# Retention attention and a routed expert layer in one kernel: order of loads, list reads and weight splits around the passage between them

## The chip, the cores and the metric

One core of a Trainium2 chip runs the whole program. The metric is the time of one execution in microseconds (us) of device time, lower is better. TensorE (PE in the profile) multiplies, PEld is its weight load, VectorE is DVE, ScalarE is ACT, GpSimd is POOL, SyncE is SP and issues most of the DMAs.

## What is computed

A decayed linear attention over 4 batches, 8 heads, 768 positions and 64 features; then each of the 3072 tokens goes to one of 16 experts, a two-layer network of width 1024, chosen by a group and then within the group:

```python
state = gamma * state + einsum('bhd,bhe->bhde', k[:, :, t], v[:, :, t])
y[:, :, t] = scale * einsum('bhd,bhde->bhe', q[:, :, t], state)
x = y.transpose(0, 2, 1, 3).reshape(B * S, H * D)
g = argmax(x @ w_group)
e = argmax(x @ w_expert[g])
out = softmax_weight(g) * softmax_weight(e) * (relu(x @ w1[g, e]) @ w2[g, e])
```

## The kernel before

**Attention** is twelve steps (`NS2`), the loop of `attention` (L901). A step i takes 128 positions of two batches and handles its operands as chunks. It has these TensorE groups: the scores of step i+1 (`score_mm`, L227, tile `sh`), the part of the outputs from the running state (`state_out`, L278, tile `op`), the part from the values (`value_out`, L291), the state update (`state_mm`, L253, tile `stp`, from the scaled values `vs` and the transposed keys `kk`), the router's logits of step i-1 (`logits_mm`, L310) and the transposes of that step's x (`trans_mm`, L322), which ScalarE copies to `xr` (L329) and SP writes to `xd` in HBM (L332). VectorE masks the scores (L239) and scales the outputs with the decays `gx` to `xt` (`out_x`, L303). The decays of the first position block come by DMA (`decay_load`, L190), those of later ones are made by GpSimd from the ones before (L195). GpSimd also scales the values (`vprep`, L187).

In steps 9 and 10 the transposed keys of the next step aren't made by TensorE but loaded (`KEYED`, L204), into a tile with one buffer, so the load waits until the state update of the step itself is done. All loads, the writes of x and the reads of lists are issued in the order of the program on SP's one queue, and each may wait there.

**Routing** (`route`, L335) runs for batches of four chunks, cut in pieces by `yield` which `route_steps` places between the attention's groups: argmaxes and one-hot rows `oh` on VectorE (L358 to L374, with one exponential on ScalarE, L362), the ranks by TensorE (L399, L401), slots from the ranks (L407 to L419), and the tokens' weights (`weights`, L382 to L394, into `src`). `enlist` (L440) then has GpSimd write each chunk's tokens to the lists `meta` in HBM by an indirect DMA. The lists of experts 0 and 1 are cut in two: an early part, complete after twelve chunks, and the rest.

**Experts** come in "units". The four static ones are `ua` and `va` (early lists of experts 0 and 1) and `ub`, `vb` (their later tokens, same weights); 14 units for the experts in order of their list's length follow. For each, `listed` reads the list (L630, SP, tile `mt`), `gather` gets the tokens (L640, GpSimd, tile `xg`), `xtrans` transposes them (L658, tile `tpx`) and splits them into an fp16 part on ScalarE (L660) and a bf16 rest on VectorE (L661); `layers` multiplies with three products for each pair of parts (L681, tile `hps`; L713 and others, tile `yps`) and `scatter` writes the rows out (L814). Weights are loaded as f32 (`wload`, or in quarter tiles `wload_part`, L604, tile `wf`) and split by `wsplit`: high part `wh` on ScalarE (L616), rest `wl` on VectorE or, for `ua`, on GpSimd (L618).

**What sets the order.** The schedule is manual: every engine runs its instructions in the order in which the Python code emits them. `attention` calls `beside(i, place)` at five places of a step, place -1 at its head, 0 after the decays, 2 ahead of the values' outputs, 1 after the outputs are scaled, 3 after the transposes of x; and `extra(i)` at its end. `beside` holds what is done for the experts during the attention: loads of `ua`'s and `va`'s parts, the early lists' reads (step 9), their gathers (step 10), the transposes of `ua` (step 11) and some splits. `NEXT` says which quarter tiles of `va` are loaded in which step. After the loop `run` (L1056 to L1094) emits the passage: last logits, three low splits, `first(2)` (the first pieces of `ua`'s layers, which `self.first` holds), the last x, the last batch's routing, ranks between further pieces of `ua`, the remaining list entries, the transposes of `va`, the reads of the later lists, the ordering of the experts (`order`, L451) and then `va`, `ub`, `vb`, during which the transposes of `ub` wait for its gather.

PSUM has banks by tag: `big` (three), `tra`, `mid` (two), `sta`, `log`. The four attention banks `sh` are the three `big` and the `tra` one; `sta` holds the running state until step 10, and serves unit transposes later.

## Time and profile before

| | us |
|---|---|
| median of 3 runs | 429.47 |
| lowest, highest | 427.44, 431.81 |
| profiled execution | 429.22 |
| its span, first to last instruction | 427.5 |
| TensorE busy in the span | 407.7 |
| VectorE, ScalarE, GpSimd busy | 289.3, 223.5, 176.4 |

The profile is of one execution. The span is what the trace covers; the execution's own time is 1.7 us longer. A busy TensorE is not TensorE at its peak, since the ends of matmuls are modelled. Idle time of an engine that nothing waits for costs nothing. [...]

### The profile page before, as it was taken

Reading aid. Unit: us, or ns where it says so; the run is one execution under the profiler, and the core shown is the slowest. Engines: PE = TensorE matmul, PEld = TensorE weight load, DVE = VectorE, ACT = ScalarE, POOL = GpSimd, SP = SyncE. Lnnn points to the kernel's source line nnn. Section 1 sums busy time; section 2 is a strip of 40 time slices with the busy share of each in tenths; the row PEclk is TensorE's granted clock in tenths of the full one; section 3 lists DMA queues with packets and bytes.
Section 4 is the critical chain, followed back from the end, with each engine's and each line's share of the span. In section 5 each row is a group of like instructions: output and inputs, shape, how many; then the busy total and the mean of one; then the engine's idle time right before and its main releaser. Section 6 shows DMA issues by size and latency. Waiting matters only on the chain.

```text
span 427.5 us, 13524 instructions
## 1 busy us (share of the span) xinstructions
PE 407.7 (95%) x5721; PEld 335.3 (78%) x5721; DVE 289.3 (68%) x473; ACT 223.5 (52%) x342; POOL 176.4 (41%) x153
## 2 busy tenths in 40 slices
PE   8899999899898999999999999999999999999991
PEld 4798989787765778585979788897978879878791
DVE  4455675578683557676898786867768778687620
ACT  2134435445523556555556566666766657667520
POOL 4445679648877021440508052442513415222001
PEclk9999999999999999999999999999999999999997
DMA  8999999998445967776776876879778797786000
GB/s 277 366 306 314 379 310 322 350 251 265 164 102 191 340 250 229 247 260 233 254 245 219 281 269 244 291 256 282 267 288 286 272 299 280 278 321 241 26 9 34
DMA packets 36913, 107.94 MB, mean 253 GB/s; under 512 B 13784, under 2 KB 13784, under 8 KB 29684
## 3 DMA queue, kind: packets, MB, share of 16 engines
q1 hardware_dynamic: 25908, 89.76, 62.1%
q0 software_dynamic: 10944, 17.31, 11.6%
q8 instruction: 45, 0.74, 0.7%
q14 instruction: 16, 0.13, 0.1%
HBM read 94.65 MB, written 13.77 MB: 254 GB/s over the span
## 4 chain that ended last, share of the span: by engine, by line
PE 62%; issue 20%; DMA 6%; POOL 6%; DVE 2%; ACT 1%; SPq 0%; POOLq 0%; ACTq 0%; DVEq 0%
PE hps L681 21%; PE yps L713 8%; PE yps L759 7%; PE yps L761 5%; PE op L291 4%; PE sh L227 3%; POOL out L814 3%; PE op L278 2%; DMA gx<-dec 2%; PE tpx L658 2%; PE sh L310 2%; POOL xg L640 2%; PE sh L322 2%; PE stp L253 2%; PE sh L212 1%
## 5 line engine op out<-in xcount | busy, mean ns | idle before, releaser
L618 DVE TENSOR_TENSOR wl<-wf,wh 128x1024 bf16<-128x1024 f32 x120 | 147.6, 1240 | 40.2 <-ACT wh L616 32.6
L681 PE MATMUL hps<-xbh,wh 128*128 128x128 f16 (+14 forms) x576 | 134.3, 245 | 0.6 <-ACT xr L329 0.6
L681 PE MATMUL hps<-xbl,wh 128*128 128x128 bf16 (+14 forms) x576 | 134.2, 245 | 0.4 <-issue 0.3
L616 ACT ACTIVATE wh<-wf 128x1024 f16<-128x1024 f32 (+1 forms) x136 | 133.4, 1001 | 1.6 <-DMA wf<-w1p 1.6
L681 PE MATMUL hps<-xbh,wl 128*128 128x128 f16 (+14 forms) x576 | 134.2, 245 | 0.0
L814 POOL DMA_INDIRECT out<-yo,mt x32 | 41.9, 1310 | 180.8 <-ACT yo L796 152.3
L681 PEld LDWEIGHTS <-wh 128*128 128x128 f16 x1152 | 102.6, 98 | 4.6 <-issue 1.9
L640 POOL DMA_INDIRECT xg<-xd,mt x32 | 53.5, 1673 | 25.5 <-DMA mt<-meta 14.9
L686 ACT ACTIVATE hh<-hps 128x256 f16<-128x256 f32 (+14 forms) x72 | 35.0, 488 | 52.7 <-PE hps L681 50.9
L761 PEld LDWEIGHTS <-wh 128*128 128x128 f16 x704 | 44.7, 98 | 21.0
L681 PEld LDWEIGHTS <-wl 128*128 128x128 bf16 x576 | 56.3, 98 | 1.0 <-issue 0.3
L239 DVE TENSOR_TENSOR pf<-sh,cst 128x512 f32<-128x512 f32 x48 | 30.8, 684 | 29.4 <-PE sh L227 13.3
L689 DVE SCALAR_TENSOR_TENSOR hl<-hps,hh 128x256 bf16<-128x256 f32 (+14 forms) x69 | 38.0, 553 | 17.0 <-ACT hh L686 14.5
L660 ACT ACTIVATE xbh<-tpx 128x512 f16<-128x512 f32 (+13 forms) x32 | 16.9, 527 | 47.6 <-PE tpx L658 47.3
L187 POOL TENSOR_TENSOR vs<-lv,cst 128x512 f32<-128x512 f32 x24 | 24.5, 1046 | 22.1 <-DMA lv<-qkv 11.4
L759 PE MATMUL yps<-wh,hh 128*128 128x512 f16 x88 | 33.4, 380 | 0.0
L759 PE MATMUL yps<-wl,hh 128*128 128x512 bf16 x88 | 33.4, 379 | 0.0
L759 PE MATMUL yps<-wh,hl 128*128 128x512 f16 x88 | 33.4, 379 | 0.0
L661 DVE TENSOR_TENSOR xbl<-tpx,xbh 128x512 bf16<-128x512 f32 (+13 forms) x32 | 19.2, 601 | 20.8 <-ACT xbh L660 20.8
L440 POOL DMA_INDIRECT meta<-src,slot x24 | 26.5, 1103 | 14.8 <-DVE src L394 6.4
L761 PEld LDWEIGHTS <-wl 128*128 128x128 bf16 x352 | 23.1, 98 | 10.4
L761 PE MATMUL yps<-hl,wh 128*128 128x103 bf16 (+10 forms) x352 | 26.3, 197 | 0.0
(146 smaller groups left out, 611.1 us busy)
## 6 DMA issues: line engine op xcount, KB each, us to landing
wf<-w1p SPq DMA_DIRECT2D x26, 1024.0 KB
wf<-w2p SPq DMA_DIRECT2D x26, 1024.0 KB
xd<-xr SPq DMA_DIRECT2D x12, 512.0 KB
lq<-qkv SPq DMA_DIRECT2D x11, 512.0 KB
lk<-qkv SPq DMA_DIRECT2D x11, 512.0 KB
lv<-qkv SPq DMA_DIRECT2D x11, 512.0 KB
wf<-w1p SPq DMA_DIRECT2D x16, 256.0 KB
wf<-w2p SPq DMA_DIRECT2D x16, 256.0 KB
```

Of the source, the lines that this page charges most:

```text
L239: nc.vector.tensor_tensor(o, sc, tri, ALU.mult)
L440: i = nc.gpsimd.indirect_dma_start(out=self.metaf, out_offset=bass.IndirectOffsetOnAxis(ap=slot[:, c:c + 1], axis=0), in_=src[:, c, :], in ...
L616: nc.scalar.activation(u["wh"][i][:, cs], u["wf"][i][:, cs], AF.Copy)
L618: (eng or nc.vector).tensor_tensor(u["wl"][i][:, cs], u["wf"][i][:, cs], u["wh"][i][:, cs], ALU.subtract)
L640: nc.gpsimd.indirect_dma_start(out=xg[0:r, i, :], out_offset=None, in_=self.xd[0:n, :], in_offset=bass.IndirectOffsetOnAxis(ap=mt[0:r, i, ...
L681: nc.tensor.matmul(hv[:, a, 0:W], l[:, k, fs], r[:, k, 0:W], start=(n == 0), stop=(n == 11))
L686: nc.scalar.activation(hh[:, f, 0:W], hv[:, :, 0:W], AF.Relu)
L689: nc.vector.scalar_tensor_tensor(*rest)
L713: nc.tensor.matmul(ps[0:r, :], l[:, k, ts], m[k], start=(n == 0), stop=(n == 23))
L759: nc.tensor.matmul(big, h[:, k, 0:P], w[k], start=(n == 0), stop=(n == 23))
L761: nc.tensor.matmul(yv[:, d, 0:r], w[k][:, d * P:d * P + P], h[:, k, P:P + r], start=(n == 0 and d == 0), stop=(n == 23), skip_group_check= ...
L814: s = nc.gpsimd.indirect_dma_start(out=self.out, out_offset=bass.IndirectOffsetOnAxis(ap=mt[0:r, i, 0:1].bitcast(U32), axis=0), in_=yo[0:r ...
```

## The change

1. The constants are loaded in two parts: the masks' triangles, value decays and state decays (308 columns) at the old place, the rest (263 columns) by a DMA of its own behind the router's weights. The strict triangle's copy to bf16 moves from the setup to the end of step 1. Readers of the second part use `self.rest`.
2. The first loads' order is changed: the decays go ahead of `q2 k2 v1`.
3. Of `va`'s quarter tiles 0 and 1 are loaded at the head of step 9, ahead of `ua`'s, and 2 and 3 at its place 3; the early lists' reads go from place 1 (ahead of the keys' load) to place 3 (behind that load, the write of x and the two quarter tiles).
4. `vprep(i + 1)` is emitted ahead of `beside(i, -1)`, so ahead of the gathers in step 10.
5. The last logits use a bank of their own (tag `sta`) instead of `sh[3]`; the last `xr` is taken from another pool, so it has its own buffer.
6. In the last routing the weights come ahead of the ranks.
7. The low part of `ua`'s tokens is taken out of `xtrans` (`xlow`) and emitted after the outputs of step 11 are scaled.
8. The splits of `va` are spread otherwise: high parts 0 (step 10), 1 (step 11, place 2), 2 (place 3), 3 (after the last x); low parts 0 (step 11, place 1), 1 (after the last logits), 2 (after the transposes of `va`), 3 to 5 (after the ordering).
9. The second gather tile is cleared by two ScalarE copies behind the last routing's first piece instead of by a GpSimd memset.

```diff
-NEXT = {9: (0, 4), 10: (4, 8), 11: (8, 12)}
+NEXT = {(9, 0): (0, 2), (9, 3): (2, 4), (10, 0): (4, 8), (11, 0): (8, 12)}
...
-        self.cst = cst = cp.tile([P, C_END], F32, name="cst")
+        self.cst = cp.tile([P, C_REST], F32, name="cst")
+        self.rest = cst = cp.tile([P, C_END], F32, name="rest")
...
-        nc.sync.dma_start(cst, self.a_cst)
+        nc.sync.dma_start(self.cst, self.a_cst[:, 0:C_REST])
...
-        nc.vector.tensor_copy(self.stri, cst[:, C_STRI:C_STRI + P])
...
-    def logits_mm(self, i, bank):
+    def logits_mm(self, i, bank=None):
...
-        lt = self.sh[bank][:, 0:2 * P]
+        lt = self.pp.tile([P, 512], F32, name="lgt", tag="sta", bufs=1) if bank is None else self.sh[bank]
+        lt = lt[:, 0:2 * P]
...
-        xr = self.wp.tile([P, 2, DM], F32, name="xr", bufs=1)
+        xr = (pool or self.wp).tile([P, 2, DM], F32, name="xr", bufs=1)
...
+        if last:
+            yield from weights()
         yield "wait"
...
         if not last:
             yield "wait"
-        yield from weights()
+            yield from weights()
...
+            u["tv", i] = tv
+            if low:
+                self.xlow(u, i)
+
+    def xlow(self, u, i):
+        r = u["rows"][i]
+        ts = slice(i * P, i * P + r)
+        self.nc.vector.tensor_tensor(u["xl"][:, :, ts], u["tv", i][:, :, 0:r], u["xh"][:, :, ts], ALU.subtract)
...
-        for o in "qB0 kB0 vA0 vB0 q1 k1 q2 k2 v1 d0 w0".split():
+        for o in "qB0 kB0 vA0 vB0 q1 k1 d0 q2 k2 v1 w0 c0".split():
...
+            elif o[0] == "c":
+                self.nc.sync.dma_start(self.rest, self.a_cst[:, C_REST:])
...
-            beside(i, -1)
             if not last:
                 self.vprep(i + 1)
+            beside(i, -1)
...
+            if i == 1:
+                self.nc.vector.tensor_copy(self.stri, self.rest[:, C_STRI:C_STRI + P])
...
+                for k in range(*NEXT.get((i, place), (0,))):
+                    self.wload_part(va, k)
...
-                if i == 9 and place == 1:
+                if i == 9 and place == 3:
                     assert self.done >= EARLY
                     self.listed(ua, "early0")
                     self.listed(va, "early1")
...
-                    for k in range(*NEXT.get(i, (0,))):
-                        self.wload_part(va, k)
                     if i == 10:
                         self.wsplit(va, 0, low=False)
-                        self.wsplit(va, 1, low=False)
-                    if last:
-                        self.wsplit(va, 0, high=False)
                 if place == 2:
                     if last:
-                        self.xtrans(ua, 'big', (0,))
-                        self.wsplit(va, 2, low=False)
+                        self.xtrans(ua, 'big', (0,), low=False)
+                        self.wsplit(va, 1, low=False)
                 if place == 1:
                     early(i - 1, 0, False)
                     if last:
-                        self.wsplit(va, 3, low=False)
+                        self.xlow(ua, 0)
+                        self.wsplit(va, 0, high=False)
+                if place == 3:
+                    if last:
+                        self.wsplit(va, 2, low=False)
...
-            nc.gpsimd.memset(self.xg[1], 0.0)
...
-            self.logits_mm(last, 3)
-            for k in (1, 2, 3):
-                self.wsplit(va, k, high=False)
+            self.logits_mm(last)
+            self.wsplit(va, 1, high=False)
             first(2)
-            self.trans_mm(last)
+            self.trans_mm(last, self.yp)
+            self.wsplit(va, 3, low=False)
...
+            for k in range(2):
+                nc.scalar.activation(self.xg[1][:, k], self.one, AF.Copy, scale=0.0)
...
+            self.wsplit(va, 2, high=False)
             self.steps.append(self.order())
...
-            self.wsplit(va, 4, high=False)
-            self.wsplit(va, 5, high=False)
+            for k in (3, 4, 5):
+                self.wsplit(va, k, high=False)
```

## Rows read from the trace of the kernel before

**Rows 1.** Busy time by stretch; columns: us, engines (instructions), PEclk, DMA share, GB/s

```profile
20.00:80.00 60.00, 59.89 (x1324) 54.36 (x1315) 37.51 (x102) 25.20 (x52) 39.14 (x38) 1.00 0.98 328
80.00:140.00 60.00, 53.26 (x810) 42.15 (x810) 39.93 (x103) 26.46 (x49) 43.95 (x41) 1.00 0.70 212
140.00:410.00 270.00, 269.69 (x3121) 219.23 (x3119) 200.55 (x248) 165.43 (x229) 83.52 (x54) 1.00 0.74 254
```

**Rows 2.** Waits of TensorE, 80 to 140 us: total, times, longest

```profile
PE tpx L658 <- DMA xg<-xd,mt: 1.8, 1, 1.8
PE stp L253 <- issue: 1.8, 2, 1.0
PE sh L310 <- ACT xr L329: 0.9, 1, 0.9
PE hps L681 <- ACT xr L329: 0.6, 1, 0.6
```

**Rows 3.** Timeline of the start: start, us, engine, line, tiles, [idle before <- releaser]

```profile
15.45 1.44 PE L227 MATMUL sh<-lq,lk 64*64 64x128 f32 x32
...
17.15 1.29 DVE L303 TENSOR_TENSOR xt<-op,gx 128x512 f32<-128x512 f32 x2 [1.36 <-DMA gx<-dec]
...
18.59 0.99 PE L278 MATMUL op<-lq,V 64*64 64x128 f32 x27 [0.20 <-DVE xt L303]
```

**Rows 4.** Timeline of steps 9 to 11, all engines

```profile
86.08 3.86 SPq L604 DMA_DIRECT2D wf<-w1p  x4
...
90.44 1.03 SPq L630 DMA_DIRECT2D mt<-meta  x2
...
91.58 1.31 SPq L204 DMA_DIRECT2D kk<-kt  x1
...
92.98 0.39 SPq L332 DMA_DIRECT2D xd<-xr  x1
...
96.12 1.06 ACT L616 ACTIVATE wh<-wf 128x1024 f16<-128x1024 f32 x1 [0.26 <-DMA wf<-w1p]
...
97.03 1.07 POOL L640 DMA_INDIRECT xg<-xd,mt  x1 [6.71 <-DMA mt<-meta]
...
98.20 1.15 PE L253 MATMUL stp<-vs,kk 128*64 128x64 f32 x32 [0.77 <-issue]
...
99.08 3.53 DVE L618 TENSOR_TENSOR wl<-wf,wh 128x1024 bf16<-128x1024 f32 x1
...
103.11 0.66 PE L658 MATMUL tpx<-ident,xg 128*128 128x128 f32 x4
```

**Rows 5.** Timeline of the passage, from the last logits to the later lists

```profile
108.27 0.23 DVE L407 TENSOR_TENSOR log<-log,nb 128x64 f32<-128x64 f32 x1 [1.50 <-PE log L326]
...
108.48 2.29 POOL L618 TENSOR_TENSOR wl<-wf,wh 128x512 bf16<-128x512 f32 x2
...
110.54 3.60 DVE L618 TENSOR_TENSOR wl<-wf,wh 128x1024 bf16<-128x1024 f32 x3
...
110.94 1.79 POOL L440 DMA_INDIRECT meta<-src,slot  x1 [0.17 <-issue]
...
114.08 1.09 ACT L329 ACTIVATE xr<-sh 128x512 f32<-128x512 f32 x2 [2.14 <-DMA xd<-xr]
...
117.57 1.18 POOL L618 TENSOR_TENSOR wl<-wf,wh 128x512 bf16<-128x512 f32 x1
...
118.11 0.23 DVE L407 TENSOR_TENSOR log<-log,nb 128x64 f32<-128x64 f32 x1 [1.53 <-PE log L401]
...
120.28 0.18 DVE L394 RECIPROCAL src<-log 128x4 f32<-128x4 f32 x1
...
120.74 1.00 POOL L440 DMA_INDIRECT meta<-src,slot  x1 [1.10 <-DVE rows L430]
...
130.16 2.06 POOL L640 DMA_INDIRECT xg<-xd,mt  x1 [2.04 <-issue]
...
134.56 0.66 PE L658 MATMUL tpx<-ident,xg 128*128 128x128 f32 x4 [1.76 <-DMA xg<-xd,mt]
```

More of the change, by code (lines that the diff above doesn't have):

```diff
@@ L44 @@
 PW = WIDTH + [P] * 4
-C_TRI, C_GV, C_GS, C_STRI, C_DESC = 0, 256, 304, 308, 436
-C_SEL = 456
-C_SEG, C_KP, C_WP, C_IT = 476, 476 + NP, 476 + 2 * NP, 476 + 3 * NP
+C_TRI, C_GV, C_GS, C_REST = 0, 256, 304, 308
+C_STRI, C_DESC, C_SEL = 0, 128, 148
+C_SEG, C_KP, C_WP, C_IT = 168, 168 + NP, 168 + 2 * NP, 168 + 3 * NP
 C_END = C_IT + MAXI
@@ L69, in constants @@
     g = 1.0 - 2.0 ** (-5.0 - np.arange(H))
-    c = np.zeros((P, C_END), np.float64)
+    c = np.zeros((P, C_REST + C_END), np.float64)
     for i in range(2):
@@ L77, in constants @@
         c[64 * half:64 * half + 64, C_GS:C_GS + 4] = g[[h[half] for h in HEAD]] ** P
-    c[:, C_STRI:C_STRI + P] = s[:, None] < s[None, :]
-    c[:, C_DESC:C_DESC + 20] = [4, 3, 2, 1] * 5
-    c[:, C_SEL:C_SEL + 20] = s[:, None] % 64 == np.arange(20)[None, :]
-    c[:, C_SEG:C_SEG + NP] = np.arange(NP) * CAP
-    c[:, C_KP:C_KP + NP] = np.arange(NP)
-    c[:, C_WP:C_WP + NP] = PW
-    c[:, C_IT:C_IT + MAXI] = np.arange(MAXI)
+    d = c[:, C_REST:]
+    d[:, C_STRI:C_STRI + P] = s[:, None] < s[None, :]
+    d[:, C_DESC:C_DESC + 20] = [4, 3, 2, 1] * 5
+    d[:, C_SEL:C_SEL + 20] = s[:, None] % 64 == np.arange(20)[None, :]
+    d[:, C_SEG:C_SEG + NP] = np.arange(NP) * CAP
+    d[:, C_KP:C_KP + NP] = np.arange(NP)
+    d[:, C_WP:C_WP + NP] = PW
+    d[:, C_IT:C_IT + MAXI] = np.arange(MAXI)
     return c.astype(np.float32)
@@ L315, in logits_mm, with trans_mm @@
         nc.scalar.activation(s["ls"], lt, AF.Copy)
-    def trans_mm(self, i):
+    def trans_mm(self, i, pool=None):
         nc, s = self.nc, self.st[i]
@@ L325, in trans_mm @@
             lg = self.log[:, a:a + 20]
-            nc.tensor.matmul(lg, s["ls"][:, u * P:u * P + P], self.cst[:, C_SEL:C_SEL + 20], start=True, stop=True)
-        xr = self.wp.tile([P, 2, DM], F32, name="xr", bufs=1)
+            nc.tensor.matmul(lg, s["ls"][:, u * P:u * P + P], self.rest[:, C_SEL:C_SEL + 20], start=True, stop=True)
+        xr = (pool or self.wp).tile([P, 2, DM], F32, name="xr", bufs=1)
         for u in range(2):
@@ L340, in route @@
         c0, n = BATCHES[i]
-        cst = self.cst
+        cst = self.rest
         def t(name, *shape, dt=F32):
@@ L451, in order @@
     def order(self):
-        nc, rp, cst = self.nc, self.rp, self.cst
+        nc, rp, cst = self.nc, self.rp, self.rest
         V = nc.vector
@@ L494, in items @@
     def items(self):
-        nc, rp, cst = self.nc, self.rp, self.cst
+        nc, rp, cst = self.nc, self.rp, self.rest
         V = nc.vector
@@ L644, in gather, with xtrans @@
             )
-    def xtrans(self, u, tag="tra", tiles=(0, 1)):
+    def xtrans(self, u, tag="tra", tiles=(0, 1), low=True):
         nc, bp, pp, W = self.nc, self.bp, self.pp, u["W"]
@@ L660, in xtrans @@
             nc.scalar.activation(xh[:, :, ts], tv[:, :, 0:r], AF.Copy)
-            nc.vector.tensor_tensor(xl[:, :, ts], tv[:, :, 0:r], xh[:, :, ts], ALU.subtract)
+            u["tv", i] = tv
[5 more added lines that the diff above has]
+        self.nc.vector.tensor_tensor(u["xl"][:, :, ts], u["tv", i][:, :, 0:r], u["xh"][:, :, ts], ALU.subtract)
     def layers(self, u):
```

## The prediction

> **What bounds the kernel now.** I read the busy shares by stage first [rows 1]. From 140 to 410 us TensorE is busy for 269.69 of 270 us, so whatever delay it brings to 140 us it carries to the end, and what is saved before 140 us is saved at the end. Between 20 and 80 us it is as full (59.89 of 60), with the DMA engines at 0.98 of their time. What is left lies in 80 to 140 us, where 6.7 us of 60 are idle, and in the first 20 us. Next I asked whom TensorE waits for in 80:140 [rows 2]: the gathered tokens (tpx), the state update (stp), released by nothing that the profile shows, and twice the x copy of ScalarE (xr). Then I went through the timeline of the start [rows 3], of the steps around the early lists [rows 4] and of the passage from attention to experts [rows 5]. All times below are those of the kernel before: "at 103.11" means what happens there now, and gains of earlier stages come on top.
>
> The sum is made against the profiled execution, 429.22 us, of which the span is 427.5. The median of the runs shown, 429.47, is 0.25 above it.
>
> **Start: constants in two parts, decays ahead of q2, k2, v1.** Of the constants' 2284 bytes per partition 1232 stay in the first transfer. The other 134 KB go behind the router's weights, which frees 0.4 us in front of all that follows (at 328 GB/s [rows 1]). Their first readers are the triangle's copy in step 1, one VectorE operation off TensorE's path, and the logits' selection after that. The larger piece is the decays. VectorE is done with the masks at 15.79, sits idle for 1.36 us until the decays land, and scales the outputs from 17.15; TensorE finishes its scores at 15.45 + 1.44 = 16.89 and gets on with the state's part of the next outputs at 18.59, when both scaled halves are out of its banks [rows 3]. With the decays three transfers (1.3 MB) earlier the wait goes: outputs are scaled from 15.4 to 16.7, and TensorE goes on at about 17.0. That is 1.6 us. Late next are k2 and v1, which the decays (256 KB, 0.8 us, less the 0.4) push back by 0.4; so step 2's scores eat the constants' gain, and v1's scaling on GpSimd still ends before its use. Bounds: 0.3 if k2 comes as late as the decays came, 2.0 if the constants' 0.4 is kept too.
>
> **Steps 9 and 10: keys, list reads, scaling of v.** TensorE is idle for 0.77 us ahead of the state update at 98.20. The profile shows no releaser, but the keys that it multiplies were issued at 91.58, behind the list reads and four weight parts [rows 4]. Now the list reads and two of the parts follow the keys, which are issued over 1 us earlier with 0.5 MB less in front: I take the whole 0.8 as gone. Bounds 0 and 0.8.
>
> The list reads pay for it. They were issued at 90.44. Now they follow on SP's queue the keys, the x copy of step 8 (92.98: it waits for ScalarE) and two weight parts, so they are issued at about 95.3 (92.98 + 0.39, and two parts at 3.86 / 4 each). On the ring keys and x copy, 1.05 MB, were behind them and are now in front: 3.2 us at 328 GB/s. GpSimd's gather starts when they land, at 97.03 after 6.71 us idle; so now at about 100.2. From the gather to the transposes it takes 6.1 us now (97.03 to 103.11), but TensorE hardly waited there. In the one case where TensorE did wait it took 4.4 (130.16 to 134.56 [rows 5]), which is 3.4 when that gather's own 2.06 are put at the 1.07 of this one. I take 3.4: transposes at 103.6. Without the keys' wait TensorE would be there at 102.3, so it stands for 1.3 us and is 0.5 later than before: the keys' gain is spent. Bounds: no stall (97.03 + 3.4 lies before 102.3); and 8.5 us from issue to use, which a weight part needed (the last of the row at 86.08 to the split at 96.12 [rows 4]), with 6.1 for the gather: 95.3 + 8.5 + 6.1 = 109.9, 6.8 later than before. GpSimd's scaling of v for step 11 now runs ahead of its wait for the lists; that takes about 2 us out of what is queued behind the gathers, so that its list entries catch up before 111.
>
> **Passage: own bank for the last logits, own x copy, fewer splits.** TensorE's two waits for the x copy, 0.9 and 0.6 [rows 2], go: the last logits no longer write the bank that is being copied, and the last x copy no longer waits 2.14 us for the DMA of the one before [rows 5]. But TensorE then only comes sooner to the transposes at 134.56, where it waits 1.76 us for the tokens of the second list. So the time is set by the chain of routing, list entries, list reads and gather. From the first entry of the last batch (120.74) to those transposes it is 13.8 us, which nothing in the change touches. Ahead of it:
> VectorE sits 1.50 us idle before the ranks of the batch before (108.27). The low part of the gathered tile (0.7) and one split (1.2 = 3.60 / 3) go in there, 0.4 too long. So GpSimd's four entries of that batch start 0.4 late, at 111.3. One of them took 1.79 beside VectorE's three splits, where the entry of 120.74 takes 1.00; one split instead of three gives back about 0.8. They and the split that stands at 117.57 + 1.18 = 118.75 end at 118.4. GpSimd's clearing of the gather tile, which stands between that split and the entry, goes to ScalarE: two copies as long as the x copy's (1.09), for which the 2.14 us of idle time there are the cover.
> On VectorE two splits less bring the last batch 2.4 - 0.4 = 2.0 us forward: ranks at 116.1 instead of 118.11. From there eleven operations of some 0.2 us run to 120.46, five for the slots and six for the weights. The six now run in the 1.53 us in which VectorE waits for the ranks, so slots and weights are ready at 117.2. The first entry waits for GpSimd: 118.4 instead of 120.74, so 2.35 us are won. Bounds: 0.3 (a split caught behind GpSimd, below) and 3.5 (slots alone). Splits that move behind the second list's tile delay that list's first layer, which has those same 1.76 us of TensorE's wait as its cover; when they are gone each split more costs 1.2.
>
> Why splits and GpSimd shouldn't meet: one of VectorE's took 3.53 us at 99.08, when GpSimd had begun its scaling of v [rows 4], against 1.2 elsewhere. [...]
>
> **Sum.** -1.6 (start), +0.5 (keys less list reads), -2.35 (chain) = -3.45: 429.22 - 3.45 = 425.8 us.
>
> **Rivals.**
> Lists in time: the rings drain faster, the gather starts by 98.9, and there is no stall in step 11. For it: only 0.70 of DMA time is used in 80 to 140. Against it: the reads can't be issued before 95. -1.6 - 0.8 - 2.35 gives 424.5.
> Splits against GpSimd: VectorE's new split before 108.27 falls behind GpSimd's two splits (2.29 us from 108.48 [rows 5]) and ends 2 us later, and all of the chain with it: 427.8. For it: the 3.53 us. Against it: GpSimd has v's scaling behind it by then and should be further on.
> Slower: the list reads take the 8.5 us and the gather its 6.1: -1.6 + 6.8 - 2.35 = +2.85, 432.1. The change loses from the point where step 11's transposes start later than 107.1 (103.11 + 1.6 + 2.35). For it: three large transfers in front of the reads. Against it: DMA is far from full after 100 us.
> Program supply: TensorE stops twice for 1.8 us in all before or inside the state update, with no releaser [rows 2], in a stretch with DMA near its limit. If such stops are its instructions, fetched by DMA behind the data, then the keys were never the wait, and a start that runs 1.6 us ahead meets the same full DMA queues and gives that back in longer stops. What is left: 429.22 + 0.5 - 2.35 = 427.4. [...]
>
> **How the numbers follow.** Forecast (425.8) 0.42, lists in time (424.5) 0.22, splits against GpSimd (427.8) 0.14, slower (432.1) 0.11, program supply (427.4) 0.11. One per cent is 4.3 us, about what a measurement of this kernel can tell from no change; below 425.2 counts as faster. Some 0.4 of the forecast's cases and 0.8 of the first rival's lie there, and few of the others: 0.37. Slower than 433.8 needs the slow rival and bad luck in the start: 0.07. The rest, 0.56, is within. At its slow end the range goes beyond no change and leaves out most of the slow rival's cases; at the other it takes in all bounds met together (-2.0 - 0.8 - 3.5 = -6.3, 422.9) and 1 us for runs that differ: 421.9 to 430.0.
>
> **What would show it.** Right: VectorE doesn't wait for the decays and the state's part of step 1's outputs starts near 17; the state update of step 10 follows at once; GpSimd's gather comes 2 to 4 us later against TensorE's work; TensorE waits some 1.3 us for DMA at step 11's transposes; the last batch's weights stand ahead of its ranks, and its first entry comes over 2 us sooner after those transposes; 0.5 to 2 us of waiting stay at the second list's transposes. Wrong: no wait in step 11 (then 424.5 or less) or one of over 5 us (then no gain); a split of over 2 us on VectorE ahead of the ranks; stops without releaser in 20 to 100 us of over 3 us.

## The result, and the profile after

The changed kernel takes 432.0 us in the median (429.48 to 437.3, 22 runs) where the kernel before takes 429.63 on the same chip: a ratio of 1.0059, 95% interval 1.004 to 1.0079. It is slower by 0.6%, 2.4 us. Ratios, here and below, leave out executions that fell into a slower state, at most three of a kernel's runs in one session, and so are not the quotients of the medians. The profiled execution took 432.21 us, its span is 430.5, 3.0 more than before.

Busy time by stretch of the changed kernel, columns as in [rows 1]:

```profile
20.00:80.00 60.00, 58.77 (x1295) 53.43 (x1292) 37.85 (x103) 25.08 (x52) 40.39 (x39) 1.00 0.97 332
80.00:140.00 60.00, 51.70 (x763) 41.47 (x765) 36.98 (x102) 26.31 (x49) 38.23 (x36) 0.94 0.62 190
140.00:410.00 270.00, 268.18 (x3097) 218.74 (x3123) 199.91 (x246) 165.92 (x230) 85.45 (x57) 1.00 0.75 259
```

TensorE's work is the same, so a stretch that it fills with less of it sends the rest behind. 80 to 140 us lost 1.6 us (53.26 before), and it is the one of the three whose granted clock is below 1. 20 to 80 us lost 1.1: there went what the start had won. The difference in 140 to 410 is no further delay: the later lists' transposes come 2.94 us later than before (137.50 against 134.56), and TensorE's end 3.0.

TensorE's waits from 80 to 140 us, changed kernel; they answer to [rows 2]:

```profile
PE tpx L662 <- DMA xg<-xd,mt: 5.8, 2, 5.5
PE log L403 <- DVE src L396: 1.4, 1, 1.4
```

The two waits for the x copy are gone, as they should. But the tokens of step 11 are waited for 5.5 us in one piece, and the ranks wait 1.4 us for the weights that now stand ahead of them. The timeline of the list reads shows where the 5.5 come from (start, us, engine, line, tiles, idle before and its releaser; it answers to [rows 4]):

```profile
89.61 0.33 SPq L205 DMA_DIRECT2D kk<-kt  x1
...
92.64 1.24 SPq L608 DMA_DIRECT2D wf<-w1p  x2
93.99 1.94 SPq L634 DMA_DIRECT2D mt<-meta  x2
95.97 2.00 SPq L608 DMA_DIRECT2D wf<-w1p  x4
...
96.19 1.10 PE L254 MATMUL stp<-vs,kk 128*64 128x64 f32 x32
...
99.88 1.07 POOL L644 DMA_INDIRECT xg<-xd,mt  x1 [7.72 <-DMA mt<-meta]
...
106.10 1.11 PE L662 MATMUL tpx<-ident,xg 128*128 128x128 f32 x4 [5.52 <-DMA xg<-xd,mt]
107.14 3.68 PE L292 MATMUL op<-pf,vs 128*64 128x128 f32 x32
```

From the reads' issue to the gather 5.9 us, from the gather to the transposes 6.2. The last row is the second half of the damage: the 32 outputs of step 11 take 3.68 us where they took 1.97 before (103.70 to 105.67). The granted clock says why; columns as above:

```profile
100.00:103.00 3.00, 0.58 (x24) 0.33 (x13) 1.23 (x6) 1.08 (x3) 2.39 (x3) 1.00 0.97 327
...
104.50:111.35 6.85, 5.25 (x40) 4.66 (x42) 1.17 (x2) 1.54 (x2) 5.86 (x6) 0.50 0.41 151
111.35:118.00 6.65, 6.65 (x84) 5.64 (x81) 5.86 (x18) 4.55 (x9) 1.73 (x1) 1.00 0.22 81
```

TensorE had hardly anything to do from 100.6; the clock is at 0.50 of full speed from 104.5 to 111.35 and back at 1.00 after that. The first row also shows the DMA engines at 0.97 while the gather was under way.

The low clock is not this execution's alone. Each run has its mean granted clock on record, 0.994 in the profile before and 0.986 here. It is below 0.99 in 29 of the 34 runs of the changed kernel (these 22 and the 12 of `d_after_again`), and in 44 of the 147 runs of the kernel before that were timed beside the experiments.

At the start the wait for the decays is gone, and what it gave is soon lost:

```profile
15.85 1.28 DVE L304 TENSOR_TENSOR xt<-op,gx 128x512 f32<-128x512 f32 x2
16.29 1.03 PE L228 MATMUL sh<-lq,lk 64*64 64x128 f32 x29 [0.83 <-DMA lk<-qkv]
...
17.10 0.27 PE L279 MATMUL op<-lq,V 64*64 64x128 f32 x1
...
17.21 1.05 PE L279 MATMUL op<-lq,V 64*64 64x128 f32 x28
...
18.98 1.97 PE L292 MATMUL op<-pf,vs 128*64 128x128 f32 x32
...
21.67 1.15 PE L254 MATMUL stp<-vs,kk 128*64 128x64 f32 x32 [0.73 <-issue]
```

The state's part of the outputs starts at 17.1 instead of 17.99 and goes on at once, where it had a stop until 18.59; the values' part starts at 18.98 instead of 20.29: 1.3 us ahead. The state update behind it stops for something that the profile doesn't name, and is only 0.4 ahead (22.08 before); the values' part of step 8 is at 77.40 against 77.56.

In marks of TensorE: the outputs of step 10 come 1.1 us earlier than before (94.39, 95.47), those of step 11 come 3.4 later (107.14, 103.70), and from there to the later lists' transposes it takes 30.4 us instead of 30.9. 3.44 - 0.50 = 2.94.

### The profile page after: what moved, and what is told of

It is laid out like the page before. It is cut to its first block, busy times and chain, and to the rows that moved or that the text cites. A ratio compares the mean times of both kernels' runs of the same rounds, so it can differ in the third digit from the quotient of the medians.

```text
span 430.5 us, 13496 instructions
## 1 busy us (share of the span) xinstructions
PE 407.0 (95%) x5692; PEld 337.1 (78%) x5721; DVE 287.0 (67%) x473; ACT 224.3 (52%) x344; POOL 173.6 (40%) x152
## 4 chain that ended last, share of the span: by engine, by line
PE 62%; issue 21%; POOL 7%; DMA 5%; SPq 2%; ACT 0%; DVE 0%; POOLq 0%; ACTq 0%
PE hps L692 21%; PE yps L724 8%; PE yps L770 7%; PE yps L772 6%; PE op L292 4%; PE sh L228 4%; POOL out L825 3%; DMA lk<-qkv 2%; PE sh L312 2%; PE stp L254 2%; PE op L279 2%; POOL xg L644 2%; PE sh L324 2%; PE tpx L662 2%; DMA meta<-src,slot 2%
## 5 line engine op out<-in xcount | busy, mean ns | idle before, releaser
L622 DVE TENSOR_TENSOR wl<-wf,wh 128x1024 bf16<-128x1024 f32 x120 | 145.3, 1220 | 39.7 <-ACT wh L620 37.3
L240 DVE TENSOR_TENSOR pf<-sh,cst 128x512 f32<-128x512 f32 x48 | 30.8, 685 | 32.9 <-PE sh L228 17.1
L444 POOL DMA_INDIRECT meta<-src,slot x24 | 24.6, 1026 | 20.5 <-DVE src L396 11.3
L772 PE MATMUL yps<-hh,wl 128*128 128x103 f16 (+10 forms) x352 | 26.3, 197 | 1.2
```

The source lines that it names most:

```text
L240: nc.vector.tensor_tensor(o, sc, tri, ALU.mult)
L622: (eng or nc.vector).tensor_tensor(u["wl"][i][:, cs], u["wf"][i][:, cs], u["wh"][i][:, cs], ALU.subtract)
L772: nc.tensor.matmul(yv[:, d, 0:r], w[k][:, d * P:d * P + P], h[:, k, P:P + r], start=(n == 0 and d == 0), stop=(n == 23), skip_group_check= ...
```

## The experiments

Each was timed beside runs of the kernel before on its own chip; ratios are to those. Two runs of one kernel on different chips (below) came out half a per cent apart, so ratios from different sessions are only read together with the trace. Each trace is of one execution, whose time lies up to 2.9 us from its kernel's median.

### The list reads

`b1_lists_late`: the kernel before with item 3 of the change alone (keys first, list reads and two weight parts behind them).

```diff
-NEXT = {9: (0, 4), 10: (4, 8), 11: (8, 12)}
+NEXT = {(9, 0): (0, 2), (9, 3): (2, 4), (10, 0): (4, 8), (11, 0): (8, 12)}
...
-                if i == 9 and place == 1:
+                if i == 9 and place == 3:
```

> The kernel before with only the list reads moved to place 3 of step 9, behind the keys, the write of x and two quarter tiles (with the quarter tiles' own move). Theory: TensorE comes to step 11's transposes at about 102.3 and waits until about 107, 4 to 5 us, and the clock falls after it: 429.6 + 3 to 6 = 432.6 to 435.6, slower than the changed kernel, since the gains of the other parts are missing. Rival (the list reads are not what costs): within 1 of 429.6.

Measured: 431.8 us, ratio 1.0056 (1.0021 to 1.009). So this one item alone is slower by as much as the whole change, though by less than I expected. Its profile shows little of the reason. The tokens are waited for 3.0 us in all (first line), but only 1.0 of it at step 11's transposes (second line); the other 2.0 are at the later lists', where the kernel before has 1.8, and the clock doesn't fall with the wait (1.00 from 101 to 105 us, and 1.97 us for the outputs behind it):

```profile
PE tpx L658 <- DMA xg<-xd,mt: 3.0, 2, 2.0
...
104.64 0.66 PE L658 MATMUL tpx<-ident,xg 128*128 128x128 f32 x4 [1.02 <-DMA xg<-xd,mt]
```

From the outputs of step 8 to those of step 11 it takes 26.0 us (79.23 to 105.22), where the kernel before takes 26.1. This execution was 1.7 us late at step 8 already, with a granted clock of 0.76 from 20.3 to 27.5. So what the item costs is measured; that the wait in step 11 is what costs it isn't shown here.

`a1_lists_first`: the changed kernel with the list reads back at place 1.

```diff
-                if i == 9 and place == 3:
+                if i == 9 and place == 1:
```

> The changed kernel with one thing undone: the early lists are read at place 1 of step 9 again, ahead of the keys' load; the quarter tiles 2 and 3 stay behind the keys. Theory (the late list reads cost the change its gain): TensorE's wait of 5.5 us at step 11's transposes falls under 0.5, the granted clock stays at its upper level around it, and the time falls from 432.0 by 4 to 7 to 425 to 428, under the kernel before. Rival (the wait only moves, to the keys or to the later lists): a wait of 1 us or more for the keys in step 10 or of over 3 us at the later lists' transposes, and 430 or more.

Measured: 430.51 us, 1.0023 (0.9991 to 1.0055). The wait for the tokens and the low clock are gone (the outputs of step 11 take 1.97 us, and the run's mean granted clock is 0.995), and from the outputs of step 11 to the later transposes it takes 28.35 us (110.18 to 138.53), 2.5 less than before. But the gain that should show then doesn't: neither the 425 to 428 us of the theory nor the waits of the rival came. The profile is of the slowest of the twelve runs (433.26), and 4.0 us late at the outputs of step 8 already (81.44, 77.40 in the changed kernel). In step 10, with the gathers back at 97.77, TensorE stops again and again until 103.5, with no releaser, beside the gathers and the list entries behind them, and ScalarE's copy of the state comes late:

```profile
100.54 0.45 PE L292 MATMUL op<-pf,vs 128*64 128x128 f32 x3 [0.16 <-issue]
...
102.77 0.53 PE L292 MATMUL op<-pf,vs 128*64 128x128 f32 x5 [0.28 <-issue]
...
107.08 0.60 ACT L264 ACTIVATE V<-stp 128x512 f32<-128x512 f32 x1 [8.54 <-PE sh L324]
```

`c_pool`: the changed kernel, list reads on GpSimd's own queue right ahead of the gathers.

```diff
...
                 if place == -1 and i == 10:
...
+                    self.listed(ua, "early0", nc.gpsimd)
+                    self.listed(va, "early1", nc.gpsimd)
                     self.gather(ua)
...
-                if i == 9 and place == 3:
...
```

> The changed kernel with the two early lists read by DMAs of GpSimd's own queue, just ahead of their gathers in step 10, instead of by SP's behind keys, x and quarter tiles. Theory (the reads are late because they lie behind three large transfers in SP's ring): the gather starts within 4 us of GpSimd's issue of the reads, TensorE's wait at step 11's transposes falls under 1 us with the keys still ahead, and the time falls by 2 to 5 below the changed kernel. Rival (the DMA engines are full whatever the ring): the gather starts 6 us or more after the issue and the wait stays at 3 us or more.

Measured: 430.08 us, 1.0016 (0.9984 to 1.0047). Neither forecast came as it stood. Reads issued at 93.47 reach the gather at 98.51, 5.0 us, so another queue doesn't make them quick; but they aren't behind SP's waits any more. Step 11's transposes stop for 1.8 us, for nothing that the profile names, and the clock stays up (1.97 us for the outputs behind it, 0.994 in the mean of the run):

```profile
104.34 0.65 PE L662 MATMUL tpx<-ident,xg 128*128 128x128 f32 x4 [1.82 <-issue]
```

`a2_dummy_work`: the changed kernel with 26 idle matmuls ahead of step 11's transposes, to keep the clock up.

```diff
                 if place == 2:
                     if last:
+                        self.heat(26)
                         self.xtrans(ua, 'big', (0,), low=False)
```

> The changed kernel with 26 matmuls of ones (128x512 bf16, 0.21 us each, 5.6 us) ahead of step 11's transposes, so that TensorE is busy in its wait for the gathered tokens; they compute nothing that is used. Theory (the wait costs twice: itself, and the lower clock that follows it): outputs of step 11 take 1.97 us again instead of 3.68, the clock stays up, and the time falls by 1.5 to 3 to 429 to 430.5. Rival (the lower clock is hidden by the list chain that follows): the outputs take 1.97 again and the time stays within 0.8 of 432.0.

Measured: 433.53 us, 1.0104 (1.0046 to 1.0162). The idle matmuls take 5.83 us, the clock is 1.00 from 80 to 140 us, the outputs of step 11 come at 107.49 and take 1.97 us, the later transposes 28.6 us after them instead of 30.4. The profile, of a run of 431.4 us, has the 1.8 us that the clock had cost; the median doesn't have them and lies above both forecasts, so work put into the wait was no cure here.

`f_room`: the changed kernel with step 10's four weight parts loaded at its place 3.

```diff
-NEXT = {(9, 0): (0, 2), (9, 3): (2, 4), (10, 0): (4, 8), (11, 0): (8, 12)}
+NEXT = {(9, 0): (0, 2), (9, 3): (2, 4), (10, 3): (4, 8), (11, 0): (8, 12)}
```

> The changed kernel with the four weight parts of step 10 loaded at the end of that step instead of after the decays, so that the gathers' tokens don't share the rings with 1 MB of weights. If the weights make the gather slow, gather to transposes falls from 6.2 to about 3.5 us, the wait for the tokens in step 11 from 5.8 to 3 or less, and the ratio to the kernel before from 1.006 to about 1.000. If the gather itself takes its 6 us, wait and ratio stay.

Measured: 429.1 us, 1.0002 (0.9968 to 1.0036): by the ratio the loss is gone (over all twelve runs the median is 0.3% above that of the kernel before, 427.94), but not by the way expected. The gather still takes 5.7 us to the transposes (100.27 to 105.94):

```profile
PE tpx L662 <- DMA xg<-xd,mt: 5.0, 2, 4.7
```

and the stretches show that the edit did not clear the rings: it moved the 1 MB from ahead of the gather to right behind it (issued from 101.01):

```profile
97.00:100.00 3.00, 3.00 (x34) 2.10 (x30) 0.46 (x1) 1.50 (x4) 0.00 (x0) 1.00 0.11 32
100.00:103.00 3.00, 1.22 (x34) 0.95 (x33) 1.59 (x7) 1.73 (x5) 2.12 (x3) 1.00 0.50 170
103.00:106.00 3.00, 0.06 (x1) 0.06 (x1) 0.01 (x1) 0.00 (x0) 2.69 (x3) 0.90 0.90 194
```

Whether a gather on empty rings would have come in the 3.4 us that I took stays open. The list reads took 6.9 us to the gather (93.41 to 100.27), although the DMA engines had little to do for the last three of them (0.11, first row), so full rings alone don't explain their time. Nor is it shown where the 0.6% came back; its mean granted clock is 0.991 against 0.986, and the later transposes come 28.6 us after the outputs.

`d_after_again`: the changed kernel once more, in another session.

> The changed kernel once more, for a second profile of it and for the comparison on this chip: 430.5 to 434, TensorE's wait at step 11's transposes 2.5 to 6 us. If its stops without releaser come at the same instructions as in the first profile (the state update of step 1, of step 5, of step 8) but with other lengths, they are the program's and not the data's.

Measured: 431.81 us, 1.0058 (1.0028 to 1.0088). The longest wait for the tokens is 3.2 us this time, with the clock again at 0.50 behind it (103.9 to 107.3). The stops without releaser in the state updates of steps 1 and 8 come again, with other lengths: 1.4 and 0.3 us, where the first profile has 0.7 and 0.15.

### The start

`c_start`: the kernel before with items 1 and 2 alone.

```diff
...
-        for o in "qB0 kB0 vA0 vB0 q1 k1 q2 k2 v1 d0 w0".split():
+        for o in "qB0 kB0 vA0 vB0 q1 k1 d0 q2 k2 v1 w0 c0".split():
...
```

> The kernel before with the edits of the start alone (constants in two parts, decays ahead of q2, k2, v1, the triangle's copy in step 1). Theory (the start's gain is taken back by stops of TensorE without releaser, at each 256th of its instructions): outputs of step 1 begin 1 to 1.6 us sooner than at 20.3, a stop of about 1 follows in the state update of step 1, and by the outputs of step 8 no more than 0.5 of it is left; the time is within 1 of the kernel before. Rival (the gain is kept): step 8 is 1.3 or more ahead and the time falls by 1 to 2.

Measured: 429.63 us, 1.0005 (0.9981 to 1.0029). The values' part of step 1 comes at 18.93, 1.36 us ahead of before, that of step 2 at 28.61, 0.09 ahead, that of step 8 at 77.53, 0.03 ahead. The state update of step 1 stops for 0.73 us as in the changed kernel.

### The passage

`c_passage`: the kernel before with items 4 to 9 alone.

> The kernel before with the edits of the passage alone (order of the scaling of v and the gathers, own logits bank, own x copy, weights ahead of ranks, low part and splits moved, clearing on ScalarE); start, keys, quarter tiles and list reads as before. Theory (the passage's edits are worth what was forecast, and start and list reads ate it): from the outputs of step 11 to the later lists' transposes 28 to 29 us instead of 30.9, and the time falls by 1.5 to 3 below the kernel before of the same chip. Rival (the passage's chain has another wait in it): the stretch keeps over 30 us and the time stays within 1 of the kernel before.

Measured: 430.53 us, 1.0035 (1.0006 to 1.0065). From the outputs of step 11 to the later transposes it takes 28.55 us (105.17 to 133.72), 2.3 less than before, just the chain's forecast; and yet the kernel isn't faster. In the profile step 10 took most of it back: from its outputs to those of step 11 it takes 9.87 us where it took 8.23. Its timeline around the gathers:

```profile
96.09 1.08 POOL L643 DMA_INDIRECT xg<-xd,mt  x1 [4.14 <-DMA mt<-meta]
97.10 1.42 PE L253 MATMUL stp<-vs,kk 128*64 128x64 f32 x31
97.47 1.03 POOL L643 DMA_INDIRECT xg<-xd,mt  x1 [0.31 <-issue]
...
98.95 0.24 PE L253 MATMUL stp<-vs,kk 128*64 128x64 f32 x1 [0.44 <-issue]
98.96 2.12 PE L311 MATMUL sh<-xt,wr 128*64 128x256 f32 x8
...
102.07 0.60 ACT L263 ACTIVATE V<-stp 128x512 f32<-128x512 f32 x1 [7.16 <-PE sh L311]
```

The update ended at 99.2, but ScalarE, with nothing else to do, copied the state only at 102.07; before it did so at 100.00.

That is not all of the loss. The profile is of the fastest of the twelve runs (428.55), and at the later transposes it is still 0.8 us ahead of the kernel before (133.72, 134.56). In seven of the twelve the mean granted clock is below 0.99, and these take 431.9 us on average where the other five take 429.7; what brings the clock down in them isn't shown.

`a3_ranks_first` (the changed kernel) and `e_weights_back` (`c_passage`): the last batch's weights behind its ranks again.

```diff
-        if last:
-            yield from weights()
         yield "wait"
...
-            yield from weights()
+        yield from weights()
```

> The changed kernel with the last batch's weights behind its ranks again. Theory (the rank matmul waits for the last of the weights, which write the same bank): its wait falls from 1.4 to under 0.5 us, but the list entries then wait for the weights behind the slots, so the first entry starts only 0 to 0.5 sooner and the time stays within 0.7 of 432.0. Rival (the added wait of 1.4 us is paid in full): 430.6 or less.

> The passage edits alone, with the last batch's weights behind its ranks again. Theory B: the wait of the ranks for VectorE (1.4 us) goes and the ratio falls to about 0.999 to 1.000. Theory A and C: the weights then stand between slots and list entry again, the wait at the later lists' transposes grows by what the ranks' wait loses, and the ratio stays at 1.002 to 1.005.

Measured: 433.24 us, 1.0109 (1.0048 to 1.017), and 432.47 us, 1.0052 (1.0015 to 1.0089). The ranks' wait goes, and the stretch behind the outputs of step 11 grows to 31.1 and 30.5 us. Of these at least 1.2 and 0.75 are the lower clock's, which the outputs themselves show (3.15 and 2.72 us for 1.97; the clock is 0.50 from 106.3 to 109.7 in the first, 0.94 over 80 to 140 in the second), but `e_both_back` (below) has 31.1 with the clock at 1.00 over 80 to 140. So the 1.4 us that TensorE waits for the weights seem well spent; in the times the difference is inside the intervals. In the second, step 10 has the clearest stop of all: ScalarE idle for 6.94 us, the last 4.2 of them after the update's end, with nothing on the core to release it, and TensorE's logits behind it:

```profile
103.43 0.60 ACT L263 ACTIVATE V<-stp 128x512 f32<-128x512 f32 x1 [6.94 <-remote]
...
104.36 1.04 PE L327 MATMUL log<-cst,ls 128*128 128x20 f32 x4 [3.25 <-ACT ls L316]
```

`e_vprep_back`: `c_passage` with the gathers ahead of GpSimd's scaling of v again; `e_both_back`: that and the weights behind the ranks.

```diff
+            beside(i, -1)
             if not last:
                 self.vprep(i + 1)
-            beside(i, -1)
```

> The passage edits alone (own bank, own x copy, weights ahead of ranks, splits, clearing), without the scaling of v ahead of the gathers; all the passage edits together gave a ratio of 1.0035 to the kernel before although the stretch from step 11's outputs to the later lists' transposes was 2.3 us shorter. If the reordering of the gathers against the scaling is what takes the gain (theory A), value outputs of step 10 to those of step 11 are back at 8.2 us (9.9 with it) and the ratio is 0.996 or below. If it is not (theory B: the weights ahead of the ranks; theory C: neither), the ratio stays at 1.002 to 1.005.

> The passage edits alone without either: own bank, own x copy, later low part, splits elsewhere, clearing on ScalarE. Theory A: 0.996 or below. Theory B: 0.999. Theory C (the gain in the passage is real in one profile, but the stretch before or after it loses as much): 1.002 to 1.004, and from the later lists' transposes to the end nothing differs from before.

Measured: 431.1 us, 0.9999 (0.9955 to 1.0043), and 431.63 us, 1.0026 (0.9991 to 1.006). Each is some 0.3% below the kernel with the scaling ahead, inside the intervals. Update to copy of the state takes 2.0 us in both, and 5.0 and 5.4 in the two with the scaling ahead. But theory A asked for more, and it didn't come: a ratio of 0.996 or below, and 8.2 us from the outputs of step 10 to those of step 11. In `e_vprep_back` these take 9.6 (97.22 to 106.82), now with a stop of TensorE in its logits:

```profile
102.81 1.08 PE L311 MATMUL sh<-xt,wr 128*64 128x256 f32 x6 [1.58 <-issue]
```

So the order against the scaling isn't shown to be what takes the gain.

`e_banks_only` and `f_banks_again`: the kernel before with item 5 alone, timed in two sessions; `f_banks_weights`: with item 6 too.

```diff
-            self.logits_mm(last, 3)
+            self.logits_mm(last)
-            self.trans_mm(last)
+            self.trans_mm(last, self.yp)
```

> The kernel before with the last logits' own bank and the last x copy's own buffer, nothing else. The two waits of TensorE for the x copy (0.9 and 0.6 us) go in every theory. If the chain through the list entries sets the time, as I predicted, TensorE only waits longer for the tokens of the later lists (1.8 becomes 3 or more) and the ratio is 1.000; if TensorE's own work sets it, the ratio is 0.9965.

> The kernel before with the last logits' own bank and the last x copy's own buffer again (0.9975, 0.9942 to 1.0007 the first time). If these edits are worth their two waits (1.5 us), 0.9965 to 0.998 with an interval below 1. If the chain through the lists takes it back, 1.000.

> The same with the last batch's weights ahead of its ranks. If the chain through the last list entries sets the time, the wait at the later lists' transposes (1.8) falls by 1 to 1.5 and so does the time: 0.994. If the ranks' new wait for the weights (1.4 us on TensorE) costs what the chain wins: 0.9975, as without it.

Measured: 429.41 us, 0.9975 (0.9942 to 1.0007); 429.01, 1.0028 (0.9999 to 1.0058); 428.56, 0.9993 (0.9959 to 1.0027). No difference from before. The two waits for the x copy go, the ranks wait 2.2 us for VectorE in their place, and the tokens of the later lists are waited for 2.0 us as before: the chain sets the time there, though the wait for the tokens didn't grow as I expected. With the weights ahead the ranks' wait grows to 3.9 (and the clock falls, 0.94 in 80 to 140), and nothing is waited for at the tokens.

`f_direct` (`c_passage`) and `g_before_direct` (the kernel before): the early lists' gathers replaced by plain copies after the same wait for the list.

```diff
-                    self.gather(ua)
-                    self.gather(va)
+                    self.plain(ua)
+                    self.plain(va)
...
+            nc.gpsimd.tensor_copy(self.bp.tile([P, 1], I32, name="junk", bufs=2)[0:r], mt[0:r, i, 0:1])
+            nc.gpsimd.dma_start(xg[0:r, i, :], self.xd[i * P:i * P + r, :])
```

> The passage edits alone (ratio 1.0035 before), where the early lists' tokens are not gathered: the first rows of x are copied in one plain DMA per list, at the same place and after the same wait for the list. It leaves out the choice of tokens for these two lists. If the gathers hold up the engines' programs, the stops of TensorE and ScalarE in step 10 go: from the state update to ScalarE's copy of the state it takes 1.2 to 1.8 us (5.0 with the gathers), from the outputs of step 10 to those of step 11 some 8.2 (9.9), and the ratio falls to 0.998 or below. If they are only late by the DMA load or by chance, nothing of that changes beyond 0.2%.

> The kernel before with the same plain copies in place of the early lists' gathers; it leaves out the choice of tokens for these two lists. If the loss of the passage edits in step 10 comes from their order (scaling ahead, so that six indirect DMAs follow one another), the kernel before loses little to its gathers: 0.998 to 1.000. If any gather there costs as much, it falls as far as with the edits, by 0.7%: 0.993.

Measured: 426.43 us, 0.9965 (0.994 to 0.999), and 427.22 us, 0.9987 (0.9947 to 1.0027). With the passage edits the gathers cost 0.7% (1.0035 and 0.9965, from two sessions), in the kernel before 0.1%, which is inside the interval. The stops in step 10 are gone in both (1.2 us from update to copy), though TensorE there waits 1.6 us for the keys:

```profile
97.51 0.65 POOL L643 DMA_DIRECT2D xg<-xd  x1
...
99.52 1.15 PE L253 MATMUL stp<-vs,kk 128*64 128x64 f32 x32 [1.57 <-DMA kk<-kt]
...
100.72 0.60 ACT L263 ACTIVATE V<-stp 128x512 f32<-128x512 f32 x1 [3.92 <-PE stp L253]
```

`g_gather_late`: `c_passage` with the gathers behind GpSimd's split at place 1 of step 10.

```diff
-                if place == -1 and i == 10:
-                    self.gather(ua)
-                    self.gather(va)
...
                     early(i - 1, 0, False)
+                    if i == 10:
+                        self.gather(ua)
+                        self.gather(va)
```

> The passage edits with the gathers behind the outputs' scaling and GpSimd's split of step 10. If gathers during the state update cost the stops, these go (1.2 us from the update to ScalarE's copy, 5.0 before), the tokens come some 1 to 2 us later, which step 11's transposes may wait for; ratio 0.996 to 1.000. If the entries behind the gathers or chance make the stops, they move with the gathers and the ratio stays at 1.003.

Measured: 426.21 us, ratio 0.9959 (0.9922 to 0.9995). It is the one version that does all the work and beats both kernels, by 0.4% against the one before, in one session.

```profile
97.95 1.10 PE L253 MATMUL stp<-vs,kk 128*64 128x64 f32 x32
...
99.10 0.60 ACT L263 ACTIVATE V<-stp 128x512 f32<-128x512 f32 x1 [3.40 <-PE stp L253]
...
99.73 1.05 POOL L643 DMA_INDIRECT xg<-xd,mt  x1 [0.16 <-DMA wf<-w1p]
...
103.39 0.66 PE L661 MATMUL tpx<-ident,xg 128*128 128x128 f32 x4 [0.61 <-DMA xg<-xd,mt]
```

The update and the copy are over before the gathers start, and gather to transposes takes 3.7 us, with the DMA engines at 0.38 of their time from 100 to 103 (0.97 in the changed kernel). Only 0.6 us are waited for. Outputs of step 10 to those of step 11: 7.8 us; from there to the later transposes 27.8.

## Why the prediction was wrong

I forecast 425.8 us, with the bound of the range at 430.0; it came out at 432.0, as slow as the rival with the late lists said (432.1). That the number fits is partly luck: the gather took its 6.1 us, but the reads took 5.9 and not 8.5, the start's 1.6 that this rival keeps was lost, and the clock was not in it. By the steps:

**The start (-1.6)** came at its place as forecast (TensorE at 17.1 where I had 17.0), and was not kept. One step that failed is that what is ahead at 18 us stays ahead through a stretch in which TensorE is full: 0.4 us were left after one state update, 0.2 by step 8, and alone it is worth nothing (1.0005). That is the part of the program-supply rival that I gave 0.11. That the stops are late programs isn't shown, only that they have no releaser and that many lie where the program has run a certain length (below). (The three transfers that the decays passed are 1.6 MB, not 1.3, which the sum doesn't use.)

**The keys (-0.8)** came out as a number: in the changed kernel the state update of step 10 follows the outputs by 1.80 us without a wait, where it took 2.73. But the wait is gone in kernels whose keys stand as before too, 1.80 us in `c_passage` and 1.90 in `e_banks_only`:

```profile
97.08 1.97 PE L291 MATMUL op<-pf,vs 128*64 128x128 f32 x32
98.98 1.15 PE L253 MATMUL stp<-vs,kk 128*64 128x64 f32 x32
```

So it isn't shown that the earlier keys removed it, and the rival that they were never the wait stands. In `f_direct` and `g_before_direct` a wait of 1.6 us there is put down to the keys by name.

**The list reads (+1.3 of waiting)** are the step that failed most. Issued at 93.99 (I had 95.3 less the start's 1.6, so 93.7), they needed 5.9 us to the gather where I had 4.9, and the gather 6.2 where I took 3.4, the value of a gather of the passage, which ran with the DMA engines at a third of their time (0.32 from 130 to 134.5). The 6.1 that stood in the same trace for the very same gather I set aside because TensorE hardly waited there. That was the error: a time that nothing waited for was still the time that it took. My reason against it, DMA far from full after 100 us, holds for the kernel before (0.48 from 100 to 103) and not for the changed one (0.97). So the tokens came at 106.1, 4.1 later than forecast (103.6 less the start's 1.6). TensorE stood there at 100.6 as forecast, but by luck: of the start's gain 0.2 was left at the outputs of step 8, and from there to step 11's transposes TensorE gained 2.4 us where I had counted 0.8 for the keys. The wait was 5.5, not 1.3. That the reads' new place costs time is shown by `b1` (1.0056); undoing it in `a1` brought back 1.0059 to 1.0023, with intervals that overlap.

**What I left out** is the clock: in the changed kernel the wait of 5.5 us on TensorE was paid twice, with 1.7 us more for the outputs behind it, at 0.50 of full speed. `a1` and `a2`, where the outputs took 1.97 us, take 28.4 and 28.6 us for the stretch that took 30.4.

**The chain (-2.35)** was right in size: 30.9 us from step 11's outputs to the later transposes became 28.4 to 28.6 in `a1`, `a2` and `c_passage` and 29.2 in `e_vprep_back`; with the weights behind the ranks it is 30.5 to 31.1. Profiles without these edits have 29.0 (`g_before_direct`) to 31.8 (`b1`), so the gain is some 2 us, give or take one. (`c_pool`, 31.2, is an exception that I didn't follow up.) In the profile of the changed kernel itself 0.5 of it is left, 30.4 us, since the clock took 1.7. One step in it was wrong and cost little: the weights do not run in VectorE's wait for the ranks, since the ranks now wait for the weights (1.4 us) and VectorE waits as long as before (1.38). Not foreseen was that these edits alone (1.0035) lose their gain, in the profile mostly in step 10. With the gathers elsewhere the ratio is 0.9959, which points to their place; but the two ratios are from two sessions, and one kernel came out half a per cent apart in two, so it isn't shown. The parts alone (1.0005, 1.0056 and 1.0035) come to more than the whole (1.0059), by less than their intervals leave open. A reason that would fit: in the changed kernel the gathers start at 99.88, after the state update.

**Splits against GpSimd** didn't happen. VectorE's split ahead of the ranks took 1.22 us, with GpSimd idle beside it:

```profile
112.08 1.22 DVE L622 TENSOR_TENSOR wl<-wf,wh 128x1024 bf16<-128x1024 f32 x1
```

That a split and GpSimd's work hold each other up is not shown by any run here. My reading of the 3.53 us was off: that split starts at 99.08 and GpSimd's scaling, 2.04 us long, only at 99.47, so it had not begun. What made the split 2.3 us longer than the others stays open.

By the marks that I had named, a stall of over 5 us meant no gain, and it came. In the profile the account closes: 1.1 us ahead at the outputs of step 10, 4.5 lost from there to those of step 11, 0.5 won behind them, so 2.9 us late. Why the medians of `a1`, `c_pool` and `c_passage`, without that wait, aren't below the kernel before stays open.

## What to carry to other kernels

A transfer's time is read from issue to landing under the load that it will meet, also where nobody waited for it; a mean load over a long stretch, or the same transfer in a quieter place, is no substitute (here 6.2 us for a gather with the DMA engines at 0.97 of their time, where one at 0.32 had given me 3.4). `f_room` shows that load isn't all of it: its reads took 6.9 us, with the DMA engines at 0.11 of their time in the last three of them. A stall of several us on TensorE is to be priced with the low clock that followed it here (0.50 of full speed for 6.85 us after a wait of 5.5, for 3.4 after one of 3.2), and the clock on record for every run tells whether the profiled one is like the others. When loads are reordered, ask what the late one's consumer runs beside then: here the place of two gathers beside a state update went with more than the edits had won.

## What the runs showed of the hardware

**Stops that follow the program's length.** Many of TensorE's stops without releaser fall, in the profiles of different kernels, on the same counts of its instructions (matmuls and weight loads): 705, 961, 1473, 1729, 1985, 2497, 3265, 3521 and 4033, all a multiple of 256 apart (in the changed kernel 0.73 us at 21.67, after 705 of them, and 0.15 at 79.98, after 3265). Others don't: the 0.77 us ahead of the state update at 98.20, which I had put down to the keys, is at 3965, and the stops of `a1` in step 10 lie between 3894 and 3940. Their lengths differ from run to run; all of TensorE's waits without releaser up to 105 us come to 2.1 us before, 1.5 after, 6.6 in `a1`, 0.6 in `b1`. The page of the changed kernel has the program as a DMA queue of its own (packets, MB, share):

```profile
q8 instruction: 45, 0.74, 0.7%
```

That a program that arrives late causes those on the even spacing is my guess, and no run shows it. At a DMA share of 0.94 to 0.99 in 20 to 80 us the traces show single stops of up to 1.8 us (`f_room`; 1.29 at 21.86 in `a1`).

**Gathers and the copy of the state.** Time from the start of step 10's state update to ScalarE's copy of it, by where the gathers stood:

| kernel | gathers from | update | to the copy |
|---|---|---|---|
| before | 97.03 | 98.20 | 1.80 |
| c_passage | 96.09 | 97.10 | 4.97 |
| e_weights_back | 97.72 | 98.06 | 5.37 |
| e_vprep_back | 98.69 | 99.65 | 1.99 |
| f_banks_again | 95.92 | 96.27 | 1.19 |
| after | 99.88 | 96.19 | 1.15 |
| g_gather_late | 99.73 | 97.95 | 1.15 |
| f_direct (plain copies) | 97.51 | 99.52 | 1.20 |

Not every gather has a late copy beside it (1.19 us in `f_banks_again`), and the time of the run doesn't follow: the profiles of `c_passage` and `f_banks_again` are both of the fastest run of twelve. The table's long times all have a gather beside them, and plain copies of as many tokens in the same place have none. Of the profiles that it leaves out, `e_both_back` (1.97), `c_pool` (2.01) and `e_banks_only` (2.62) fit this. Two don't: in `a1` (2.86) the gathers started over four us before the update, and in `b1` (3.01) ScalarE had a split until 101.05, as the gathers began. By what means is open.
